# A sinkhorn attention and gated MLP kernel on one core: one q turned by a transposing transfer, a new order of all units, output products in halves

## The chip, the core and the metric

The kernel runs on one core of one Trainium2 chip. The metric is the device time of one execution in microseconds (us). A core has five engines with their own instruction streams: TensorE (PE in the profile, with its weight loads as PEld), VectorE (DVE), ScalarE (ACT), GpSimd (POOL) and SyncE (SP). SP, ACT and POOL also issue transfers, which sixteen DMA engines carry out. Each engine works through its own instructions in program order and waits at one whose inputs or buffers are not ready.

## What is computed

With B=4 batches, H=8 heads, S=768 tokens, D=64 and 8 blocks of 96 tokens:

```python
P = sort_net                                   # (B, H, 8, 8)
for _ in range(5):                             # P = softmax-like rows, then columns
    P = np.exp(P - P.max(-1, keepdims=True))
    P = P / (P.sum(-1, keepdims=True) + 1e-9)
    P = P / (P.sum(-2, keepdims=True) + 1e-9)
k_sorted = einsum('bhij,bhjcd->bhicd', P, k_blocks)      # blocks mixed by P; v the same
scores = scale * q_block @ k_sorted_block.T              # per block of 96 tokens
x = softmax(scores) @ v_sorted_block                     # (B, S, 512) over all heads
h = relu(x @ w_in)                                       # 512 -> 1024
u, v = h[..., :512], h[..., 512:]
v = (v - mean(v)) / sqrt(var(v) + 1e-6)
v = einsum('ts,bsd->btd', w_spatial, v) + b_spatial      # mixes tokens, 768 x 768
out = (u * v) @ w_out                                    # 512 -> 512
```

## The kernel before

All work is cut into small units, and the string ORDER (lines 18 to 51) lists them in the order in which they are issued. A unit is a name and its arguments, parted by colons; `run` calls the function `u_<name>` for each. The schedule is manual: the list is at once the order of the instructions on each engine. The framework adds the waits that data and buffers ask for. The batches overlap in the list: while one is in the MLP, the next is in attention.

The units of one batch b, in the order in which data flows (`ps` is the number 0 to 3 of a PSUM buffer, an engine letter A, D or P says who evicts or computes, hp is a pair of heads, ih a half of the tokens):

- `L:q:b`, `L:k:b`, `L:v:b`, and `L:wv`, `L:wu`, `L:wsa`, `L:wsb`, `L:wo` for the weights: loads from memory, issued by POOL, casting to bf16. `LH` loads half of the first q in fp32 over SP, and `QC` casts it on ACT. Loaded tiles and the output tiles share a ring of eight buffers (`ld`).
- `SK:0` to `SK:4`: the five normalisations on ACT and DVE. `PR`, `P0`, `PC`, `PD` spread P over the partitions, on PE, DVE, ACT or DVE, and POOL.
- `KT` (L383, 12 matmuls with 64-column weights): a pair of heads of k is mixed and turned. `VT` does the same for v of batch 0, and `VB` (L401) turns it back. For other batches `VM` (L410) mixes v into the tile `vm`, and `VC` (L423) copies four 16-row pieces into `vb` by SP transfers.
- `QT` and `QQ` (L314): one or two pairs of heads of q are turned by PE transposes, 12 or 24 with 64-column weights, and copied to `qT` by ACT or DVE.
- `SC` (L442): 8 score matmuls with 64-row weights, then an exponential on ACT (L447) into a ring of five tiles. `AT` (L488): 8 matmuls of the exponentials with `vb`, then reciprocal and product on DVE (L495, L496).
- `XT` (L518): x turned by PE transposes, or `XD` (L506): turned by one transposing transfer on SP (batches 2 and 3).
- `VP` (L554) and `UP` (L597): the two halves of `x @ w_in`, evicted with relu. `ST` (L571) statistics on DVE, `LN` on ACT, `LA` (L583) normalisation on DVE. `WW` (L531) turns the spatial weights once.
- `SP` (L609): 12 matmuls that mix tokens, then the sum with the bias on DVE (L615, tile `z`, three buffers). `GT` (L626): the gate product with u on DVE or POOL.
- `OP` (L635): two 128-token rows of the output product, `OE` evicts them, `OS` stores them. For the last batch `SH`, `GH`, `OH`, `OI`, `OJ` are smaller pieces of `SP`, `GT`, `OP`, `OE`, `OS`.
- `DM` (L226): six dummy matmuls at the start. `CK`, `CF`, `LF`: a check that all sums lie in a safe range, its flag, and the loading of that flag by the engines; behind `IF` the list's tail runs in the usual branch (else a general path, not taken here).

Two functions in the kernel are not in the list before. `QP` copies one pair of heads of q within SBUF so that both heads of a token group lie side by side, and `QX` turns them all at once:

```python
def u_QX(b, lo, hi):                                        # L368
    nc.sync.dma_start_transpose(
        out=q_tile(b)[:, lo * S:hi * S].rearrange("p (x c) -> p x c", c=128),
        in_=st["qp", b][:, lo:hi].rearrange("p k g h d -> p (k g h d)"))
```

`OP` has a last argument `parts`; with 2, each row's 512 columns are made as two products of 256 (L635): `for c in range(0, DM, w): for mc in range(FC): matmul(t[:, x, c:c + w], ...)`.

Of the kernel before, what the change touches and what calls it, by code (L numbers as in the profile page):

```python
# [15 lines left out]


ORDER = """
IV:0 CO S0 SK:0 SK:1 LH:S:0 L:q:0:4:8 L:k:0:0:8 L:v:0:0:8 SK:2 IV:2 ID MA L:v:1:0:8 MC QC:A:1 SK:3 L:k:1:0:8 MB QC:A:0
DM:0:6:512 L:q:1:0:8 DM:2:6:512 DM:1:6:512 QT:3:A:0:1 SK:4 QT:2:A:0:3 DM:0:6:512 DM:3:6:512 L:wv QT:1:A:0:0 QT:2:A:0:2  # L20
PR:0 P0:0:2 L:wu P0:6:8 P0:2:4 DM:3:6:512 P0:4:6 PC:D KT:1:D:0:1 PD:1:4:8 KT:3:A:0:0 L:wsb L:wsa KT:0:D:0:3 KT:2:A:0:2
IV:1 L:v:2:0:8 VT:1:A:0:0 VT:3:D:0:1 PD:1:0:4 SC:0:0:0:0 SC:2:0:0:1 VB:1:D:0:0 L:k:2:0:8 VB:3:D:0:1 SC:0:0:1:0
VT:1:A:0:2 AT:2:0:0:0 VT:3:A:0:3 PD:2:4:8 AT:0:0:1:0 L:q:2:0:8 VM:1:A:1:0 VB:2:D:0:2 SC:3:0:1:1 XT:0:D:0:0:0
AT:1:0:0:1 SC:2:0:2:0 VM:3:A:1:3 VB:0:D:0:3 PD:2:0:4 SC:1:0:2:1 AT:2:0:2:0 KT:3:D:1:1 KT:0:D:1:2 SC:1:0:3:0 VM:2:A:1:1
SC:3:0:3:1 AT:1:0:1:1 KT:2:A:1:3 KT:0:A:1:0 AT:3:0:3:0 VM:1:A:1:2 PD:3:4:8 QQ:2:D:1:0 XT:3:D:0:1:0 L:k:3:0:8
AT:0:0:3:1 XT:1:A:0:0:2 QQ:2:A:1:2 AT:3:0:2:1 VP:1:A:0:0:1 XT:0:D:0:1:2 ST:0:1 VP:2:D:0:2 ST:0:0 SC:0:1:1:1 SC:3:1:2:1
L:q:3:0:8 VC:1:4:8 VP:1:D:0:4:5 SC:2:1:3:1 ST:0:4 ST:0:5 SC:3:1:3:0 VP:0:A:0:3 SC:2:1:0:1 ST:0:2 UP:1:A:0:1:1
AT:0:1:1:1 L:v:3:0:8 SC:3:1:0:0 ST:0:3 UP:2:A:0:0:0 AT:0:1:3:1 AT:1:1:2:1 LN:0:0:6 UP:3:A:0:0:1 AT:0:1:0:1 LA:0:5
WW:2:A:0 WW:1:D:4 XT:3:A:1:1:2 UP:0:A:0:1:0 LA:0:2 VC:1:0:4 AT:2:1:0:0 VM:1:A:2:1 BI WW:3:D:2 SC:0:1:2:0 VM:2:A:2:2
XT:1:D:1:1:0 LA:0:0 BH LA:0:4 LA:0:1 LA:0:3 VM:3:A:2:0 SC:0:1:1:0 VP:1:A:1:4:5 AT:2:1:3:0 AT:0:1:1:0 ST:1:5 SP:3:0:2  # L30
AT:0:1:2:0 L:wo SP:1:0:0 VM:2:D:2:3 SP:0:0:1 VC:2:4:8 XT:3:D:1:0:2 XT:1:A:1:0:0 VC:2:0:4 QQ:2:D:2:0 KT:0:A:2:1
KT:3:D:2:0 GT:D:0:0 QQ:1:D:2:2 KT:2:A:2:2 KT:0:A:2:3 PD:3:0:4 GT:P:0:2 VP:3:A:1:0:1 SC:1:2:0:1 SC:2:2:0:0 SP:0:0:3
ST:1:4 SC:3:2:2:1 SC:1:2:1:1 ST:1:1 VP:2:A:1:2:3 KT:3:D:3:2 QQ:0:D:3:0 ST:1:2 SC:1:2:3:0 UP:2:A:1:1:0 AT:0:2:0:1
GT:P:0:3 KT:3:A:3:0 ST:1:3 QQ:1:D:3:2 SC:0:2:3:1 AT:2:2:2:1 UP:3:D:1:0:1 VM:1:A:3:3 UP:0:A:1:0:0 AT:2:2:3:1
UP:3:A:1:1:1 GT:P:0:1 ST:1:0 LN:1:0:6 AT:2:2:1:1 AT:0:2:3:0 XD:2:1 LA:1:4 OP:1:0:0:2 AT:2:2:0:0 OE:A:0:0 OP:0:0:2:2
SC:2:2:2:0 LA:1:2 LA:1:5 OE:D:0:2 SC:1:2:1:0 LA:1:1 LA:1:0 LA:1:3 OP:3:0:4:2 AT:1:2:1:0 AT:0:2:2:0 SP:2:1:2 VM:0:D:3:1
VM:1:D:3:0 OE:A:0:4 VP:3:D:2:4:5 KT:0:A:3:1 KT:2:D:3:3 SP:1:1:3 VM:0:A:3:2 GT:D:1:3 OS:0:0 ST:2:4 SP:3:1:1 SC:2:3:3:1
SC:1:3:1:1 XD:2:0 OS:0:2 GT:D:1:2 ST:2:5 SP:0:1:0 VC:3:4:8 SC:3:3:2:1 SC:2:3:0:1 UP:1:D:2:1:0 GT:D:1:1 VC:3:0:4
VP:3:A:2:2:3 AT:1:3:3:1 GT:P:1:0 VP:2:A:2:0:1 ST:2:3 AT:1:3:2:1 AT:3:3:1:1 UP:0:A:2:1:1 OP:1:1:0 ST:2:0 ST:2:1 ST:2:2
OE:A:1:0 AT:2:3:0:1 LN:2:0:6 LA:2:1 UP:0:D:2:0:0 SC:1:3:0:0 LA:2:3 SC:3:3:1:0 LA:2:2 LA:2:5 LA:2:0 OP:2:1:4 AT:1:3:0:0  # L40
AT:3:3:1:0 XD:3:1 OE:A:1:4 OP:0:1:2 LA:2:4 SC:1:3:3:0 OE:D:1:2 SC:3:3:2:0 SP:2:2:2 AT:1:3:2:0 UP:0:A:2:0:1 AT:3:3:3:0
CK VP:2:A:3:4:5 GT:D:2:2 OS:1:2 SP:1:2:1 ST:3:5 OS:1:4 XD:3:0 SP:3:2:3 SP:2:2:0 ST:3:4 CF:3 GT:D:2:1 GT:P:2:3
UP:0:A:3:1:0 VP:2:D:3:2:3 VP:3:A:3:0:1 ST:3:0 ST:3:1 ST:3:2 UP:2:A:3:0:1 GT:P:2:0 LF OP:1:2:2 ST:3:3 OE:A:2:2 LN:3:0:6
OP:0:2:0 LA:3:4 LA:3:5 OS:2:2 OE:A:2:0 UP:3:D:3:1:1 LA:3:2 LA:3:0 OP:2:2:4 LA:3:3 OE:A:2:4 LA:3:1 OS:2:4 UP:0:A:3:0:0
SH:1:3:3:0 GH:P:3:3:0 SH:2:3:0:0 GH:D:3:0:0 SH:0:3:1:0 SH:2:3:2:0 SH:3:3:1:1 GH:P:3:1:0 SH:1:3:0:1 GH:P:3:2:0 OS:1:0
GH:P:3:1:1 SH:2:3:3:1 SH:3:3:2:1 OS:2:0 GH:P:3:0:1 GH:D:3:2:1 GH:D:3:3:1 OS:0:4 IF OH:1:3:2:0:512:0:4
OH:2:3:3:0:512:0:4 OH:0:3:4:0:256:0:4 OI:A:3:2:0:512 OI:A:3:3:0:512 OH:3:3:5:0:256:0:4 OI:D:3:4:0:256 OI:D:3:5:0:256
OJ:3:2:0:512:S OJ:3:3:0:512:S OJ:3:4:0:256:S OJ:3:5:0:256:A OH:2:3:5:256:512:0:4 OH:1:3:1:0:512:0:4
OH:3:3:4:256:512:0:4 OI:D:3:5:256:512 OI:A:3:1:0:512 OJ:3:5:256:512:S OI:A:3:4:256:512 OJ:3:4:256:512:S OJ:3:1:0:512:A
OH:2:3:0:0:512:0:4 OI:A:3:0:0:512 OJ:3:0:0:512:S  # L50
"""


# [773 lines left out]
```

## Time and profile before

| | |
|---|---|
| time, median of 3 runs | 156.74 us (156.48 to 156.78) |
| profiled execution, its own time | 156.77 us |
| span of that execution | 155.0 us |
| PE busy | 148.5 us (96%) |
| DVE busy | 120.3 us (78%) |
| ACT busy | 81.6 us (53%) |
| POOL busy | 36.8 us (24%) |
| granted TensorE clock | 1.0 |

The span runs from the first to the last instruction of the core; the execution's time has 1.77 us around it. The profile is read through a page (busy time of each engine, the span in 40 slices, the chain of work that ended last, the costliest groups of instructions) and through views of the same trace: the chain in order of time, instructions in order of time, groups by shape, transfers with their time from issue to landing. In the group rows stand the line, engine and operation, the tiles out<-in, the count, the busy time in all, the mean of one in ns, and the engine's idle time ahead of them. PE times in the instruction rows overlap, because matmuls are pipelined; the chain's pieces do not.

### The profile page before, as it was taken

What the parts mean: (1) busy time and instruction counts of PE and PEld (TensorE: products, weight loads), DVE (VectorE), ACT (ScalarE), POOL (GpSimd) and SP (SyncE); (2) the same over time, 40 slices, a digit from 0 to 9 for tenths busy, and PEclk for the clock granted to TensorE, in tenths of its full rate; (3) what the DMA queues carried; (4) which work ended last, traced back from release to release, by engine and by line L of the source; (5) the groups of instructions that cost most, each with busy time, mean ns of one, the idle gap of its engine ahead of it and who ended that gap; (6) DMA issues with size and microseconds to landing.
All of it is one profiled execution on the core that took longest, in us unless ns stands there. A gap on an engine that the chain in (4) does not pass through costs nothing.

```text
span 155.0 us, 4028 instructions
## 1 busy us (share of the span) xinstructions
PE 148.5 (96%) x1689; PEld 92.1 (59%) x1689; DVE 120.3 (78%) x261; ACT 81.6 (53%) x112; POOL 36.8 (24%) x43
## 2 busy tenths in 40 slices
PE   6999898999999999999999999999999999999990
...
GB/s 72 267 203 204 205 204 205 208 217 238 271 217 203 203 204 204 242 226 16 0 17 224 43 198 64 147 1 4 102 148 185 44 0 0 131 49 371 141 226 183
DMA packets 27653, 23.57 MB, mean 152 GB/s; under 512 B 7280, under 2 KB 24688, under 8 KB 27632
## 3 DMA queue, kind: packets, MB, share of 16 engines
...
q10 hardware_dynamic: 288, 0.39, 0.7%
q8 instruction: 14, 0.23, 0.6%
...
## 4 chain that ended last, share of the span: by engine, by line
PE 93%; ACT 3%; DVE 1%; issue 1%; DVEq 0%; ACTq 0%
PE ps L609 15%; PE ps L554 14%; PE ps L597 14%; PE ps L635 10%; PE ps L226 7%; PE ps L488 5%; PE ps L665 5%; PE ps L442 4%; PE ps L383 4%; PE ps L314 4%; PE ps L685 3%; PE ps L410 2%; PE ps L518 2%; PE ps L531 1%; PE ps L401 1%; ACT kt_all L115 1%
## 5 line engine op out<-in xcount | busy, mean ns | idle before, releaser
L447 ACT ACTIVATE ex_all<-ps 96x768 bf16<-96x768 f32 x32 | 24.8, 805 | 8.7 <-PE ps L442 8.6
L626 POOL TENSOR_TENSOR gt<-z,u_sb 128x768 bf16<-128x768 f32 x6 | 9.8, 1642 | 78.6 <-DVE z L615 61.3
L609 PE MATMUL ps<-wspT,v_sb 128*128 128x384 bf16 x144 | 25.1, 326 | 0.0
L597 PE MATMUL ps<-xT,w_in_sb 128*128 128x384 bf16 x128 | 23.5, 326 | 0.0
L554 PE MATMUL ps<-w_in_sb,xT 128*128 128x512 bf16 x96 | 22.9, 380 | 0.2 <-issue 0.2
L496 DVE TENSOR_TENSOR x_sb<-ps,rec_all 96x512 bf16<-96x512 f32 x32 | 22.0, 687 | 1.1
L609 PEld LDWEIGHTS <-v_sb 128*128 128x128 bf16 x144 | 13.5, 98 | 8.9
L571 DVE BATCH_NORM_STATS2 stats<-v_sb 128x6 f32<-128x512 bf16 x24 | 16.3, 678 | 2.0 <-ACT v_sb L121 1.5
L115 ACT COPY o_sb<-ps 128x1024 f32<-128x1024 f32 (+2 forms) x12 | 9.7, 816 | 15.2 <-PE ps L685 10.2
L635 PE MATMUL ps<-w_out_sb,gt 128*128 128x256 bf16 (+1 forms) x96 | 16.9, 326 | 0.0
L615 DVE TENSOR_TENSOR z<-ps,b_bc 128x768 f32<-128x768 f32 x12 | 11.4, 952 | 7.0 <-PE ps L609 6.8
L121 ACT ACTIVATE u_sb<-ps 128x768 bf16<-128x768 f32 x12 | 9.7, 810 | 13.1 <-PE ps L597 13.0
L597 PEld LDWEIGHTS <-w_in_sb 128*128 128x128 bf16 x128 | 11.6, 98 | 7.4
L554 PEld LDWEIGHTS <-xT 128*128 128x128 bf16 x96 | 8.6, 98 | 9.7 <-issue 0.7
L121 ACT ACTIVATE v_sb<-ps 128x1024 bf16<-128x1024 f32 (+1 forms) x9 | 8.8, 976 | 9.1 <-PE ps L554 9.1
L488 PEld LDWEIGHTS <-ex_all 96*128 96x128 bf16 x256 | 10.6, 97 | 3.7 <-issue 0.6
L488 PE MATMUL ps<-vb,ex_all 96*128 96x65 bf16 x256 | 12.2, 193 | 0.5 <-issue 0.5
L635 PEld LDWEIGHTS <-gt 128*128 128x128 bf16 x96 | 9.0, 98 | 5.5
L226 PE MATMUL ps<-warm 128*128 128x512 bf16 x36 | 10.7, 461 | 1.3 <-DVE warm L201 1.3
L115 ACT CAST kt_all<-ps 128x768 bf16<-128x768 f32 x9 | 6.9, 800 | 6.5 <-PE ps L383 6.5
L442 PE MATMUL ps<-qT,kt_all 64*128 64x96 bf16 x256 | 9.3, 204 | 0.4 <-DVE kt_all L117 0.4
L495 DVE RECIPROCAL rec_all<-ps 96x8 f32<-96x8 f32 x32 | 6.3, 196 | 4.3 <-PE ps L488 4.0
...
## 6 DMA issues: line engine op xcount, KB each, us to landing
...
k_in<-in_k_dram POOLq DMA_DIRECT2D x4, 768.0 KB, 23.2
v_in<-in_v_dram POOLq DMA_DIRECT2D x4, 768.0 KB, 22.3
vb<-vm SPq DMA_DIRECT2D x24, 99.0 KB, 5.8
q_in<-in_q_dram POOLq DMA_DIRECT2D x3, 768.0 KB, 29.8
...
q<-in_q_dram SPq DMA_DIRECT2D x1, 768.0 KB, 4.6
```

What stands on the lines that cost most here:

```text
L115: nc.scalar.copy(out=out, in_=in_)
L121: nc.scalar.activation(out=out, in_=in_, func=AF.Relu)
L226: nc.tensor.matmul(t[:, 0, 0:int(w)], lhsT=warm[:, 0:128], rhs=warm[:, 0:int(w)], start=True, stop=True)
L442: nc.tensor.matmul(t[:, hh, 0:HW].rearrange("p (g x) -> p g x", g=G)[:, :, ii * TB:(ii + 1) * TB], lhsT=kT[rows, i * BLK:i * BLK + 128], r ...
L447: nc.scalar.activation(out=e_tile(b, hp, ih).rearrange("p h (x g) -> p h x g", g=G), in_=t[0:BLK, :, 0:HW].rearrange("p h (g x) -> p h x g ...
L488: nc.tensor.matmul(t[:, hh, ii * VW:ii * VW + D + 1], lhsT=e[:, c:c + 128], rhs=vb[b % 2][:, ih * NI + ii, 2 * hp + hh, 0:D + 1], start=Tr ...
L496: nc.vector.tensor_mul(out=x_sb[:, hp].rearrange("p i (h d) -> p h i d", h=2), in0=tv[:, :, :, 0:D], in1=_raw_ap(rec, 0, [rec.ap[0], [NI, ...
L554: nc.tensor.matmul(t[:, x, :], lhsT=st["xT", b][:, n // 3, kc, (n % 3) * 128:(n % 3 + 1) * 128], rhs=w_in_sb[:, kc, DH:DFF], start=(kc == ...
L571: nc.vector.bn_stats(out=stats, in_=st["v_sb", b, n])
L597: nc.tensor.matmul(t[:, x, 0:HW], lhsT=w_in_sb[:, kc, mc * 128:(mc + 1) * 128], rhs=st["xT", b][:, ih, kc, :], start=(kc == 0), stop=(kc = ...
L609: nc.tensor.matmul(t[:, x, 0:HW], lhsT=st["v_sb", b, n][:, mc * 128:(mc + 1) * 128], rhs=wspT[:, 3 * x:3 * x + 3, n, :], start=(n == 0), s ...
L635: nc.tensor.matmul(t[:, x, c:c + w], lhsT=st["gt", b, mc][:, (n0 + x) * 128:(n0 + x + 1) * 128], rhs=w_out_sb[:, mc, c:c + w], start=(mc = ...
```

## The change

Only the list changes. Batch 3's q is no longer turned by `QQ:0:D:3:0` and `QQ:1:D:3:2`; four `QP:A:3:*` on ACT and one `QX:3:0:4` on SP take their place. All nine `OP` units have parts=2 (before, the three of batch 0). All other units remain, in a new order, many with another PSUM buffer or engine: of the gate products `GT`, ten are on POOL and two on DVE (before six and six), of the `GH` seven and one (before five and three), of the `KT` evictions twelve on ACT and four on DVE (before nine and seven). The q, k, v loads come in another order as well.

```diff
-IV:0 CO S0 SK:0 SK:1 LH:S:0 L:q:0:4:8 L:k:0:0:8 L:v:0:0:8 SK:2 IV:2 ID MA L:v:1:0:8 MC QC:A:1 SK:3 L:k:1:0:8 MB QC:A:0
-DM:0:6:512 L:q:1:0:8 DM:2:6:512 DM:1:6:512 QT:3:A:0:1 SK:4 QT:2:A:0:3 DM:0:6:512 DM:3:6:512 L:wv QT:1:A:0:0 QT:2:A:0:2
-PR:0 P0:0:2 L:wu P0:6:8 P0:2:4 DM:3:6:512 P0:4:6 PC:D KT:1:D:0:1 PD:1:4:8 KT:3:A:0:0 L:wsb L:wsa KT:0:D:0:3 KT:2:A:0:2
...
+S0 CO LH:S:0 SK:0 L:q:0:4:8 SK:1 IV:0 SK:2 L:v:0:0:8 QC:A:0 SK:3 DM:0:6:512 DM:1:6:512 L:k:0:0:8 ID L:k:1:0:8 MC
+L:v:1:0:8 SK:4 DM:3:6:512 DM:0:6:512 L:q:1:0:8 MA L:wv QT:3:A:0:0 QC:A:1 BH QT:0:A:0:3 IV:2 DM:1:6:512 L:wu QT:2:A:0:2
+L:wsb MB IV:1 PR:1 P0:6:8 DM:3:6:512 P0:0:2 P0:2:4 P0:4:6 L:wsa PC:A PD:1:4:8 PD:1:0:4 VT:0:A:0:0 QT:3:D:0:1 L:k:2:0:8
+VT:1:A:0:1 VB:0:D:0:0 VT:2:A:0:2 KT:3:A:0:2 VB:1:D:0:1 KT:2:D:0:3 VT:0:A:0:3 SC:3:0:2:0 L:v:2:0:8 VB:1:D:0:2
+SC:2:0:3:0 VB:0:D:0:3 KT:3:A:0:1 SC:1:0:2:1 KT:2:D:1:3 KT:3:A:0:0 L:q:2:0:8 KT:0:D:1:2 KT:1:A:1:1 AT:2:0:2:0
+SC:3:0:0:1 PD:2:4:8 AT:0:0:3:0 SC:1:0:3:1 SC:2:0:1:1 AT:3:0:0:1 SC:1:0:1:0 AT:0:0:3:1 PD:2:0:4 AT:2:0:2:1 VM:3:A:1:0
+VM:1:A:1:1 VM:0:D:1:3 KT:2:A:1:0 AT:3:0:1:1 L:q:3:0:8 VM:1:A:1:2 L:k:3:0:8 XT:0:A:0:1:2 QQ:2:D:1:2 SC:1:0:0:0
+QQ:3:D:1:0 XT:0:A:0:1:0 PD:3:4:8 AT:1:0:0:0 L:v:3:0:8 SC:2:1:2:0 SC:3:1:0:1 VP:0:A:0:3 AT:1:0:1:0 SC:2:1:3:0
+VP:3:D:0:4:5 XT:2:D:0:0:2 VC:1:0:4 XT:0:A:0:0:0 UP:1:A:0:0:1 ST:0:5 VC:1:4:8 ST:0:4 SC:3:1:1:0 VP:2:A:0:0:1 ST:0:3
+AT:0:1:3:0 AT:1:1:1:0 VP:3:A:0:2 ST:0:0 UP:2:A:0:0:0 ST:0:2 SC:0:1:0:0 AT:3:1:2:0 UP:1:A:0:1:1 ST:0:1 LN:0:0:6
+WW:2:D:2 SC:3:1:3:1 AT:0:1:0:1 LA:0:2 LA:0:4 LA:0:0 LA:0:1 WW:1:A:4 UP:2:A:0:1:0 AT:3:1:0:0 KT:0:A:2:3 WW:1:D:0
+KT:2:A:2:2 KT:0:D:2:1 SC:3:1:2:1 XT:1:D:1:0:2 KT:2:A:2:0 XT:0:D:1:0:0 VM:3:D:2:0 VM:1:A:2:2 LA:0:3 LA:0:5 BI
+VM:2:A:2:1 VP:0:A:1:0:1 AT:3:1:2:1 AT:2:1:3:1 SP:1:0:1 VM:2:A:2:3 QQ:0:D:2:0 L:wo XT:3:D:1:1:2 SC:1:1:1:1 QQ:2:A:2:2
+SC:0:2:1:1 QP:A:3:2 QP:A:3:0 AT:3:1:1:1 SP:1:0:3 XT:3:A:1:1:0 GT:P:0:1 SP:0:0:0 VC:2:4:8 SC:3:2:2:0 SC:2:2:3:1
+VP:1:D:1:4:5 SC:2:2:1:0 ST:1:4 SC:0:2:0:1 ST:1:5 ST:1:1 VC:2:0:4 PD:3:0:4 UP:3:A:1:0:1 GT:D:0:0 SP:1:0:2 KT:2:A:3:2
+GT:P:0:2 KT:3:A:3:3 UP:0:D:1:1:0 QP:A:3:1 VM:2:A:3:0 VM:1:A:3:2 ST:1:0 VP:3:A:1:2:3 GT:P:0:3 QP:A:3:3 QX:3:0:4
+AT:1:2:1:0 AT:0:2:3:1 UP:2:A:1:1:1 AT:1:2:2:0 VM:3:A:3:3 ST:1:3 OP:0:0:0:2 ST:1:2 AT:1:2:1:1 OE:A:0:0 LN:1:0:6
+UP:2:A:1:0:0 AT:0:2:0:1 VM:3:A:3:1 OP:1:0:2:2 SC:2:2:2:1 LA:1:4 VC:3:4:8 LA:1:3 SC:3:2:3:0 LA:1:1 LA:1:0 LA:1:5
+OP:0:0:4:2 OE:D:0:2 OE:A:0:4 LA:1:2 AT:2:2:2:1 SC:1:2:0:0 XD:2:1 SP:3:1:0 KT:1:A:3:0 KT:0:A:3:1 SP:2:1:2 AT:1:2:3:0
+AT:3:2:0:0 SP:0:1:1 SC:1:3:0:1 SC:2:3:1:1 VP:3:D:2:4:5 GT:P:1:0 ST:2:4 SC:0:3:2:1 SC:2:3:1:0 VC:3:0:4 XD:2:0 SP:1:1:3
...
+XD:3:1 OP:1:1:4:2 LA:2:1 OE:D:1:2 AT:2:3:0:0 AT:3:3:2:0 OE:A:1:4 SP:0:2:0 GT:P:2:0 AT:3:3:3:0 SP:1:2:3 VP:2:A:3:4:5
+SP:0:2:2 XD:3:0 UP:3:D:3:0:1 ST:3:5 CK VP:1:A:3:0:1 SP:2:2:1 VP:3:A:3:2:3 ST:3:4 CF:2 ST:3:3 GT:P:2:3 ST:3:0 GT:P:2:2
+ST:3:2 ST:3:1 OS:1:2 UP:0:A:3:1:1 GT:P:2:1 LF OP:3:2:4:2 LN:3:0:6 LA:3:2 OP:0:2:0:2 UP:1:A:3:1:0 OP:2:2:2:2 OE:D:2:4
...
+SH:3:3:3:1 SH:1:3:1:1 GH:P:3:1:1 GH:P:3:3:1 OS:2:0 IF OH:0:3:2:0:512:0:4 OH:3:3:3:0:512:0:4 OI:A:3:2:0:512
...
+OJ:3:1:0:512:S OJ:3:5:256:512:A OI:D:3:4:256:512 OH:2:3:4:0:256:0:4 OI:D:3:4:0:256 OJ:3:5:0:256:S OJ:3:4:256:512:A
+OJ:3:4:0:256:A
```

More of the change, by code (lines that the diff above doesn't have):

```diff
@@ L24 @@
[L24 to L48, printed above, removed]
```

11 lines of the change are left out of this document (7 added, 4 removed).

## The prediction

> **What bounds the kernel now.** I read the page first (busy shares, then the 40 slices), then the chain of waits in order of time, then the instructions of the stretches where that chain leaves TensorE (PE).
>
> ```profile
> span 155.0 us, 4028 instructions
> ...
> PE 148.5 (96%) x1689; PEld 92.1 (59%) x1689; DVE 120.3 (78%) x261; ACT 81.6 (53%) x112; POOL 36.8 (24%) x43
> ...
> PE   6999898999999999999999999999999999999990
> ...
> PE 93%; ACT 3%; DVE 1%; issue 1%; DVEq 0%; ACTq 0%
> ```
>
> The first row is the span, the next the busy times; in the slices PE has a hole only at both ends and around the fourth and sixth slice; the last row gives it 93% of the chain. So a unit's time on PE counts in full, and other engines count only where PE waits for them. The chain shows the places:
>
> ```profile
> 12.33 1.40 PE ps L226 x6
> ...
> 14.57 1.50 ACT kt_all L115 x2
> ...
> 25.49 0.81 ACT ex_all L447
> ...
> 33.71 0.34 PE ps L518 x8
> ...
> 40.30 0.24 PE ps L488 x8
> ...
> 61.16 0.67 PE ps L314 x24
> ...
> 71.93 0.24 PE ps L488 x8
> ...
> 73.29 0.28 PE ps L442 x8
> 73.57 0.35 PE ps L488 x8
> 73.92 1.30 PE ps L597 x8
> ...
> 78.88 1.75 PE ps L635 x16
> ...
> 104.69 1.73 PE ps L635 x8
> ...
> 130.57 3.45 PE ps L635 x16
> ...
> 146.15 5.21 PE ps L685 x32
> 151.37 0.02 issue
> 151.39 0.58 ACT o_sb L115
> ```
>
> Columns are start, length, engine and line. Until 27 us evictions on ACT and DVE alternate with PE; from there to 151.37 every piece is PE. Two things are read off for the sum. A unit has a fixed price (eight L488 matmuls 0.24, a 24-matmul q turn 0.67, eight L597 1.30). And a change between the units with 64-row or 64-column weights (L383 and L314, or L442) and the rest costs 0.11 more: L488 takes 0.24 at 71.93, but 0.35 at 73.57, straight behind L442. The Trainium skill, "TensorEngine Tiling (Array Packing)", Key Properties, says that changing the tiling mode drains the TensorE; the two L488 rows agree, and no figure is taken from the page.
>
> I add these prices in the order of the list and call the sum ahead of a unit its position. For the list before, XT:0:D:0:1:2 has position 27.47 and starts at 33.71 (offset 6.24); the first OH has 139.68 and starts at 146.15 (6.47). Over 112 us the addition and the trace differ by 0.23, so the same addition for the new list is worth having.
>
> **The change, part by part.**
>
> *Two double q turns leave PE.* QQ:0:D:3:0 and QQ:1:D:3:2 are 24 transposes each: 2 x 0.67 = -1.34.
>
> *Output products in halves.* Three of nine are in halves already: 1.75 for 16 matmuls (78.88) against 1.73 for 8 (104.69). Six more: 6 x 0.02 = +0.12. Nothing else hangs on a half, since the four products of each half read the same tiles in the same order.
>
> *New order.* Counting the changes of weight shape along both lists gives 65 before and 72 after: 7 x 0.11 = +0.77. All other PE units are the same in kind and number, the 36 dummy matmuls included. So the positions end at 144.86 before and 144.41 after: **-0.45**, a third of what the removed turns seemed to give.
>
> *What the turn needs instead.* Four QP copies on ACT, one transposing transfer on SP, one more tile of the eight-deep load ring.
>
> ```profile
> L117 DVE COPY qT<-ps 128x1536 bf16<-128x1536 bf16 x5 | 4.7, 948 | 0.3 <-PE ps L314 0.2
> ...
> L115 ACT COPY qT<-ps 128x768 bf16<-128x768 bf16 x4 | 3.1, 789 | 1.4 <-PE ps L314 1.4
> ```
> ```profile
> xT<-x_sb SPq DMA_TRANSPOSE x4, 3.8
> ```
> ```profile
> 117.73 1.65 SPq L506 DMA_TRANSPOSE xT<-x_sb  x1
> ```
>
> A QP copies 128x768 bf16 within SBUF, which no row shows; the nearest is 789 ns from PSUM, so 4 x 0.79 = 3.2 us of ACT, while DVE loses two evictions of 948 ns. Neither is on the path: ACT is busy 53% of the span. QX moves 128x3072 elements where an XD moves 96x2048, twice as many: between 3.8 us and 2 x 3.8 = 7.6, of which up to 2 x 1.65 = 3.3 block SP; I take 7.6. By positions, QP:A:3:3 can start at 69 and the first score of batch 3, SC:1:3:0:1, is at 86.16: 17 us of PE work cover it. What stands behind QX on SP (VC:3:4:8) waits for VM:3:A:3:1 at position 73.9 anyway. If that cover were gone, the whole 7.6 would show. Cost 0. The Trainium skill, "VectorE: DVE Perf Modes", The three transpose paths, speaks against the transfer: 390 ns for a 128x128 block on TensorE, 1309 ns through the DMA, and the advice to use TensorE where PSUM will do. At 24 blocks in a row it would make 31 us, an estimate from that page, and PE would wait 31 - 17 = 14.
>
> The ring tile takes the slot of the spatial weights, whose last transposition (WW:1:A:4, position 38.9) lies 14 us ahead of the first QP: 0.
>
> *The q load must be there when ACT comes to QP.* ACT would stand still otherwise, and every eviction behind it.
>
> ```profile
> 29.76 0.94 POOL L171 DMA_DIRECT2D k_in<-in_k_dram  x1
> ```
> ```profile
> k_in<-in_k_dram POOLq DMA_DIRECT2D x1, 768.0 KB, 28.0
> ```
>
> The fourteenth load of the queue landed at 29.76 + 28.0 = 57.8 (the rate is that of the queue, so the place in the order decides). In the new list q of batch 3 is the fourteenth. QP:A:3:2 comes on ACT behind the eviction of QQ:2:A:2:2 (PE done at position 52.5) and an exponential, at 54.7, near 61: 3 us to spare, cost 0.
>
> *Head (to 34 us).* The value turns come first, and 24 evictions stand on ACT from VT:0:A:0:0 to the score SC:3:1:0:1.
>
> ```profile
> 20.26 0.80 ACT L115 CAST vT<-ps 128x768 bf16<-128x768 f32 x1 [0.47 <-PE ps L383]
> 20.95 0.81 ACT L115 CAST vm<-ps 128x768 bf16<-128x768 f32 x1
> ```
> ```profile
> 13.40:33.00 19.60, 18.00 (x392) 13.83 (x391) 16.55 (x31) 16.15 (x21) 11.71 (x13) 1.00 1.29 206
> ```
>
> Each lasts 0.80, but the next begins 0.69 later when it is ready, so 24 take between 24 x 0.70 = 16.8 and 24 x 0.80 = 19.2; before, this stretch held 21 on ACT (busy 16.15 us) and 31 instructions on DVE. One q turn fewer stands ahead of PR, so the first VT starts at 12.33 + 1.40 - 0.34 = 13.4, its eviction at 13.9. Following PE, ACT and DVE unit by unit with these steps, and the PSUM buffers, ACT is the last in nearly every wait and itself waits 2.3 to 2.6 us for PE: VP:3:D:0:4:5 (position 27.11) starts at 13.9 + 16.8 + 2.3 = 33.0, up to 33.3, an offset of 5.9 to 6.2 against 6.24. Ends: without any of those waits 30.7 (3.6), at 0.80 an eviction with half of them 34.2 (7.1). I take 6.0, from the 0.69 row: **-0.24**.
>
> *Three places where the new list is tight.* (a) The value copies of batch 1:
>
> ```profile
> 29.90 0.72 SPq L423 DMA_DIRECT2D vb<-vm  x1
> ```
> ```profile
> 31.95 1.24 SPq L423 DMA_DIRECT2D vb<-vm  x2
> ```
> ```profile
> vb<-vm SPq DMA_DIRECT2D x2, 99.0 KB, 8.0
> ```
>
> The fourth transfer, issued at 31.95, lands 8.0 later, at 39.95, and the first reader ran at 40.30 (chain). Now VM:1:A:1:2 is evicted near 28.9, the fourth lands near 39.0, and AT:0:1:3:0 (position 33.04) comes at 39.0: 0 to 0.4, I take 0.1. (b) Positions 41 to 46: KT and WW of different shapes follow each other on the same PSUM buffers, with only 0.10 to 0.54 between the end of an eviction and the next writer; the tightest before were 0.05 and 0.10. 0 to 0.5, I take 0.2. (c) The end of batch 2:
>
> ```profile
> 122.40 0.96 DVE L615 TENSOR_TENSOR z<-ps,b_bc 128x768 f32<-128x768 f32 x1
> 123.53 1.64 POOL L626 TENSOR_TENSOR gt<-z,u_sb 128x768 bf16<-128x768 f32 x1 [22.88 <-DVE z L615]
> ```
> ```profile
> 126.20 0.14 DVE L727 CAST flag<-ends 1x1 int32<-1x1 f32 x1
> ...
> 133.33 0.69 DVE L571 BATCH_NORM_STATS2 stats<-v_sb 128x6 f32<-128x512 bf16 x1 [0.46 <-issue]
> ```
>
> All four gates are now on POOL. SP:2:2:1 ends at position 120.45; 0.96 and 1.64 and two hand-overs of 0.1 later, at 123.3, the last gate is there, and OP:3:2:4:2 wants it at 123.58. The flag, 4.2 us ahead of its reader before (126.34 to 130.57), is written near 122.8, and reading it (0.46 on DVE) ends near 123.3 too. 0 to 0.7, I take 0.1. Together **+0.40**.
>
> *Tail.*
>
> ```profile
> 152.00 0.33 SPq L697 DMA_DIRECT2D out_dram<-o_sb  x1
> ```
> ```profile
> L115 ACT COPY o_sb<-ps 128x512 f32<-128x512 f32 x4 | 2.3, 585 | 10.2 <-PE ps L685 10.2
> ...
> L117 DVE COPY o_sb<-ps 128x256 f32<-128x256 f32 x3 | 1.2, 425 | 0.9 <-PE ps L685 0.9
> ```
>
> The last eviction is a half row on DVE, 425 ns for 585, its store behind two others on ACT's queue: between -0.16 and +0.2, I take **-0.10**.
>
> The other moved steps (loads on POOL's queue, gates, statistics) I cost at nothing: PE is continuous there before, 50 units of the old list are marked for DVE and 36 of the new, and the least distance from an eviction to the next writer of its buffer after position 60 is 0.38 in the new list (at the OP of (c)) and 0.21 in the old.
>
> **Sum**: -0.45 - 0.24 + 0.40 - 0.10 = -0.39, against the profiled execution's 156.77 (span 155.0 and 1.77 around it): 156.38. That execution is 0.03 above the median of 156.74, so **156.4**.
>
> **The rivals.** *No new waits.* Without the 0.40 and with an offset of 5.9, 155.9. For it: DVE, the busier helper, is relieved. Against: each of the three places needs everything punctual.
> *The edges eat the saving.* Each costs double what I took: 156.8. This is no measurable change; from no change this kernel's runs (156.48 to 156.78) can tell about 0.2%, 0.31 us.
> *Slower: ACT paces the head.* Place: 14 to 33 us. If an eviction steps at 0.76 to 0.80, as when each waits for its matmul, the offset becomes 6.7 to 7.1: +0.9 in the middle, 157.3. It decides from a step of 0.76 on. For it: 21 evictions kept ACT 16.15 of 19.60 us. Against: the step of 0.69.
> *Slower: the end of batch 2.* PE waits 0.9 instead of 0.1 for gate or flag, because DVE reaches the last z late: 157.2; it decides from 0.8. For it: 0.28 us of margin where there were 4. Against: before, reading the flag left no gap on PE at 130.57.
> *The transfer is late.* It decides where its landing takes over 17 us, more than four times an XD. Against: an XD of 16 blocks of 96x128 lands in 3.8 us. By the 1309 ns a block of the Trainium skill, "VectorE: DVE Perf Modes", The three transpose paths, the time would be 156.4 + 14 = 170; 16 blocks would take 21 us there, and the measured 3.8 speaks against it.
>
> **How the numbers follow.** Forecast 0.32; no new waits 0.11; edges 0.22; ACT-paced head 0.20; end of batch 2 0.11; transfer or q late, or a wait I have not seen, 0.04. Faster 0.32 + 0.11 = 0.43, same 0.22, slower 0.20 + 0.11 + 0.04 = 0.35. The range reaches from the no-waits case with a head 0.4 faster (ACT waiting less) to both slower cases partly together: 155.5 to 157.9.
>
> **What would show it.** L314 with 48 matmuls fewer; L635 96 more of 256 columns, 48 fewer of 512; no PE wait at the first score of batch 3 and a landing of the new transfer under 8 us; VP of tiles 4 and 5 at 33.0 (34 or later means the ACT-paced head); PE waits at 39, 47 to 52 and 130 of 0.1 to 0.2. Wrong it would be by any PE gap over 0.5 us after 34, above all at OP of batch 2, or by ACT standing at the first QP.

## The result

The changed kernel takes 157.18 us (median of 20 runs, 156.69 to 158.28), the kernel before 156.52 (20 runs, 156.44 to 156.96): a ratio of 1.0045, 95% interval 1.0027 to 1.0063. It is 0.45% slower, 0.66 us; the forecast was 156.4, faster. The time lies inside the range.

The profiled execution of after took 157.20 us, that of before 156.77. From the page of after (busy times, the slices, the shares of the chain):

```profile
span 155.4 us, 4042 instructions
...
PE 147.0 (95%) x1679; PEld 96.0 (62%) x1689; DVE 110.3 (71%) x247; ACT 87.8 (56%) x122; POOL 45.9 (30%) x49
...
PE   6979988999999999999999999999999999999990
...
PE 78%; DVE 10%; ACT 6%; issue 2%; DMA 1%; DVEq 0%; ACTq 0%
```

PE is busy 1.5 us less than before, and yet the span grew by 0.4. The 1.5 us do not measure the work that went: 1.2 of them lie with the dummy matmuls at the start (10.7 us busy in before, 9.5 in after), and ten of after's matmul records are missing (1679 beside 1689 weight loads). By the positions the work fell by 0.45. The chain of waits of after, in order of time, shows where it leaves PE:

```profile
11.10 0.23 DVE p_t L252
...
25.14 0.57 issue
...
33.65 1.83 PE ps L555 x8
...
95.53 2.07 PE ps L610 x12
97.70 0.96 DVE z L616
98.66 0.12 DVE rec_all L496
98.80 0.69 DVE x_sb L497
99.49 1.70 DVE gt L627
...
102.13 0.70 DVE x_sb L497
102.87 0.35 PE ps L443 x8
...
146.33 5.21 PE ps L686 x32
151.62 0.42 DVE o_sb L118
```

Three places are to be seen: a row "issue" of 0.57 in the head, a stretch of DVE between 97.70 and 102.87 in the middle of PE's row, and the end. Laid against the positions of the prediction (VP of tiles 4 and 5 at 27.11, the SP that starts at 95.53 at 88.9, the first OH at 139.23), the offset is 33.65 - 27.11 = 6.54, then 6.63, then 7.10. So most of the 0.5 us of the body is lost between 95.5 and 103 us; on both sides of that stretch the sum of unit prices and of 0.11 us a switch holds to 0.1 us.

The account of the two profiled executions, before to after:

| part | us |
|---|---|
| PR starts sooner (11.97, then 11.47, where it waits for p_t) | -0.50 |
| PE work from PR on, by positions | -0.12 |
| stands from PR to VP of tiles 4 and 5 (before: to XT), 2.44, then 2.91 | +0.47 |
| stands from there to the first OH, 0.23, then 0.56 | +0.33 |
| from the first OH to the end of the span, 8.85, then 9.07 | +0.22 |
| sum | +0.40 |

The pieces of the chain start up to 0.16 us later than the same instructions in their own rows (146.33 and 146.17); below, where a start stands against another, both are from the same view. In the nine profiled executions of kernels with after's head PR starts between 11.47 and 11.82, so an account of two single executions is good to some tenths of a us.

### The profile page after: what moved, and what is told of

It is laid out like the page before. It is cut to its first block, busy times and chain, and to the rows that moved or that the text cites. A ratio compares the mean times of both kernels' runs of the same rounds, so it can differ in the third digit from the quotient of the medians.

```text
span 155.4 us, 4042 instructions
## 1 busy us (share of the span) xinstructions
PE 147.0 (95%) x1679; PEld 96.0 (62%) x1689; DVE 110.3 (71%) x247; ACT 87.8 (56%) x122; POOL 45.9 (30%) x49
## 4 chain that ended last, share of the span: by engine, by line
PE 78%; DVE 10%; ACT 6%; issue 2%; DMA 1%; DVEq 0%; ACTq 0%
PE ps L610 15%; PE ps L555 12%; PE ps L598 12%; PE ps L636 10%; PE ps L666 5%; PE ps L489 4%; PE ps L443 4%; PE ps L686 3%; PE ps L384 3%; ACT ex_all L448 2%; PE ps L411 2%; PE ps L315 2%; PE ps L519 2%; ACT kt_all L116 1%; PE ps L532 1%
## 5 line engine op out<-in xcount | busy, mean ns | idle before, releaser
L627 POOL TENSOR_TENSOR gt<-z,u_sb 128x768 bf16<-128x768 f32 x10 | 17.1, 1714 | 74.6 <-DVE z L616 59.4
L555 PE MATMUL ps<-w_in_sb,xT 128*128 128x512 bf16 x87 | 22.3, 380 | 0.6
L122 ACT ACTIVATE v_sb<-ps 128x1024 bf16<-128x1024 f32 (+1 forms) x10 | 9.4, 939 | 15.1 <-PE ps L555 15.1
L636 PE MATMUL ps<-w_out_sb,gt 128*128 128x256 bf16 x144 | 16.9, 273 | 0.0
L636 PEld LDWEIGHTS <-gt 128*128 128x128 bf16 x144 | 13.8, 98 | 2.2
L116 ACT COPY o_sb<-ps 128x1024 f32<-128x1024 f32 (+2 forms) x10 | 8.1, 820 | 12.5 <-issue 8.1
L122 ACT ACTIVATE u_sb<-ps 128x768 bf16<-128x768 f32 x13 | 10.6, 812 | 7.9 <-PE ps L598 7.7
L489 PEld LDWEIGHTS <-ex_all 96*128 96x128 bf16 x256 | 10.7, 97 | 4.0 <-issue 0.7
L116 ACT CAST kt_all<-ps 128x768 bf16<-128x768 f32 x12 | 9.4, 803 | 3.4 <-PE ps L384 3.3
L227 PE MATMUL ps<-warm 128*128 128x512 bf16 x35 | 9.5, 425 | 1.3 <-DVE warm L202 1.3
L443 PE MATMUL ps<-qT,kt_all 64*128 64x96 bf16 x256 | 10.0, 205 | 0.5 <-DVE x_sb L497 0.4
```

The costliest lines, as they stand in the source:

```text
L116: nc.scalar.copy(out=out, in_=in_)
L122: nc.scalar.activation(out=out, in_=in_, func=AF.Relu)
L443: nc.tensor.matmul(t[:, hh, 0:HW].rearrange("p (g x) -> p g x", g=G)[:, :, ii * TB:(ii + 1) * TB], lhsT=kT[rows, i * BLK:i * BLK + 128], r ...
L489: nc.tensor.matmul(t[:, hh, ii * VW:ii * VW + D + 1], lhsT=e[:, c:c + 128], rhs=vb[b % 2][:, ih * NI + ii, 2 * hp + hh, 0:D + 1], start=Tr ...
L555: nc.tensor.matmul(t[:, x, :], lhsT=st["xT", b][:, n // 3, kc, (n % 3) * 128:(n % 3 + 1) * 128], rhs=w_in_sb[:, kc, DH:DFF], start=(kc == ...
L627: eng.tensor_mul(out=gt, in0=st["z", b, mc], in1=u)
```

## The experiments

Ratios and medians stand against runs of the kernel before on the same chip (156.55 to 156.72 us).

**The gate product.** In after, DVE's gate of column 2 of batch 2 runs beside two gates of POOL. Instructions of after in order of time, first DVE, then POOL:

```profile
99.41 1.78 DVE L627 TENSOR_TENSOR gt<-z,u_sb 128x768 bf16<-128x768 f32 x1
```
```profile
98.73 3.95 POOL L627 TENSOR_TENSOR gt<-z,u_sb 128x768 bf16<-128x768 f32 x2 [8.47 <-DVE z L616]
```

```diff
-AT:3:3:1:1 UP:0:A:2:0:0 GT:D:1:2 GT:P:1:3
+AT:3:3:1:1 UP:0:A:2:0:0 GT:P:1:2 GT:P:1:3
```

> The kernel after with the one gate product of batch 2 that VectorE computes, column 2, given to GpSimd (its z is there from 91.4 us, so GpSimd can compute it there, alone, before the gates at 98.7 us). Theory of the gates: after's stall around 103 us comes from VectorE's gate, 1.78 us at 99.41 beside two gates of GpSimd (3.95 us at 98.73) where GpSimd's gate at 88.62 took 1.65 alone; without it GpSimd's two gates at 98.7 take 3.3 us in place of 3.95, the reciprocal now at 101.93 starts near 100.2, the scores now at 102.87 start at 102.3 to 102.5, all later positions come 0.4 to 0.5 us earlier, the time is 156.7 to 156.8. Rival, the loss between 95 and 103 us is no wait for VectorE at all: the scores stay at 102.8 to 102.9 and the time at 157.2.

Measured: 157.03 us (ratio 1.0033, 1.0014 to 1.0053). POOL computes the moved gate at 91.67, and its pair is back at its price:

```profile
98.94 3.24 POOL L627 TENSOR_TENSOR gt<-z,u_sb 128x768 bf16<-128x768 f32 x2 [5.63 <-DVE z L616]
```

The scores start at 102.60 in an execution whose head was 0.20 later; from VP of tiles 4 and 5 to the first OH it is 112.27 us in place of 112.58. So the stretch was the gates', and it is worth 0.31 us in the trace. Two kernels below that differ by this gate alone (the bias in eight transfers, without and with it) show the same, 112.58 and 112.26. Of the 0.4 to 0.5 that I expected in the time the medians show 0.15, within what they can tell. Two gates side by side cost both engines: 0.95 became 1.78 on DVE, 3.24 became 3.95 on POOL. The Trainium skill, "SBUF — State Buffer", "Who interferes with whom", says that a DVE instruction with two SBUF inputs and a GpSimd instruction that reads SBUF take turns at one shared port; these rows agree.

**The branch hint.** `BH` had moved from the middle of the list to its head, which the prediction passed over.

```diff
-QT:3:A:0:0 QC:A:1 BH QT:0:A:0:3
+QT:3:A:0:0 QC:A:1 QT:0:A:0:3
...
-VM:1:A:2:2 LA:0:3
+VM:1:A:2:2 BH LA:0:3
```

> The kernel after with the branch hint (a PE, VectorE and ScalarE instruction, at the head of the order in after) put back among the transposes of the spatial weights, where before has it. Theory of the hint: the early hint makes the 0.57 us in which PE stood at 25.14 with nothing in the profile that released it, and the spread of after's times up to 158.28; without it no such stand of over 0.3 us before 45 us, the time 156.6 to 156.8, no run over 157.5. Rival, the hint does nothing: a stand of 0.4 to 0.6 us stays in the head, the time is 157.0 to 157.3, and runs of about 158.2 still come up.

Measured: 157.26 us (ratio 1.0054, 1.0030 to 1.0078), a stand of 0.57 us at the same unit, and three of eight runs at 158.3. The hint does nothing; that theory fell. The execution profiled here was one of those of 158.3, and is used below.

**Is the head paced by evictions?** Twice: evictions moved to DVE, then taken from ACT and given to nobody.

```diff
-VT:2:A:0:2  KT:3:A:0:1  VM:1:A:1:1
+VT:2:D:0:2  KT:3:D:0:1  VM:1:D:1:1
```

> The kernel after with three evictions of the head given from ScalarE to VectorE (the mixed values of heads 4 and 5, the mixed keys of heads 2 and 3 of batch 0, the values of heads 2 and 3 of batch 1). Theory that ScalarE paces the head (it was busy 4.00 of 4.00 us in 20 to 24): ScalarE has 2.4 us less to do, the value products of token tiles 4 and 5 of batch 0, now at 33.66, start at 33.1 to 33.4, and the time is 156.7 to 156.9. Rival, the head's loss lies in PE's own stands that nothing released (0.57 us at 25.14): the value products stay within 0.15 us of 33.66 and the time within 0.2 of 157.2; with VectorE's 0.95 us for an eviction in place of 0.80 it may even be 0.2 later.

Measured: 158.24 us (ratio 1.0107, 1.0088 to 1.0127), VP of tiles 4 and 5 at 34.27. Neither theory's numbers came true: DVE is no freer there than ACT, and PE now waits for its evictions of kt_all (0.4), vm (0.4) and vT (0.3).

The second kernel copies, for KT of batch 0 and VM of batch 1 (pairs 0 and 1 of each), only a few columns; POOL sets the rest to 0 or 1 beforehand:

```diff
-copy(e, to[:, x], of[:, x])
+copy(e, to[:, 0:8], of[:, 0:8])
...
-copy(eng, vm[:, :, 2 * hp:2 * hp + 2, 0:D].rearrange(...), t[:, :, 0:G * D].rearrange(...))
+copy(eng, vm[:, 0:1, 2 * hp:2 * hp + 2, 0:D].rearrange(...), t[:, :, 0:D].rearrange(...))
```

> The kernel after, with four of ScalarE's evictions of the head (the mixed keys of heads 0 to 3 of batch 0, the values of heads 0 to 3 of batch 1) cut to a few columns: the rest of these tiles is not copied and holds constants set by GpSimd, so the outputs are not the reference's. That takes some 2 us off ScalarE between 18 and 29 us and gives them to nobody. Theory that evictions pace the head: the value products of token tiles 4 and 5 of batch 0, at 33.66 in after, start at 32.9 to 33.3, the time falls by 0.3 to 0.7. Rival, the head is paced by the arrival of loads and PE's fetching of code: 33.5 to 33.8, and the time within 0.2 us of after's 157.2.

Measured: 157.37 us (ratio 1.0061, 1.0039 to 1.0083). Busy times in 20 to 24 us (columns: stretch, length, PE, PEld, DVE, ACT, POOL, clock), after and then the lightened head, and PE's stop in each:

```profile
20.00:24.00 4.00, 3.57 (x96) 3.04 (x96) 3.25 (x6) 4.00 (x7) 0.88 (x1) 1.00 1.32 206
```
```profile
20.00:24.00 4.00, 3.46 (x96) 3.00 (x96) 3.22 (x6) 3.18 (x5) 0.88 (x1) 1.00 1.32 206
```
```profile
25.71 0.27 PE L489 MATMUL ps<-vb,ex_all 96*128 96x65 bf16 x3 [0.57 <-issue]
```
```profile
25.71 0.27 PE L494 MATMUL ps<-vb,ex_all 96*128 96x65 bf16 x3 [0.54 <-issue]
```

ACT, busy 4.00 of 4.00 before, has 0.8 us of slack now, and PE's rows agree within 0.04 us up to the stop at 25.71. Only behind it come 0.27 us (VP of tiles 4 and 5 at 33.32 against 33.59). So these four evictions pace 0.27 us of the head, all of it behind the stop, and the medians show no gain from that.

**The two parts of the change alone, in the order of before.** First the turn: four copies and one transfer in the place of the two double transposes.

```diff
-KT:3:D:3:2 QQ:0:D:3:0 ST:1:2 SC:1:2:3:0 UP:2:A:1:1:0 AT:0:2:0:1
+KT:3:D:3:2 QP:A:3:0 ST:1:2 SC:1:2:3:0 UP:2:A:1:1:0 QP:A:3:2 AT:0:2:0:1
...
-ST:1:3 QQ:1:D:3:2 SC:0:2:3:1
+ST:1:3 QP:A:3:1 SC:0:2:3:1
...
-VM:1:A:3:3 UP:0:A:1:0:0
+VM:1:A:3:3 QP:A:3:3 QX:3:0:4 UP:0:A:1:0:0
```

> The kernel before in its own order, whose two double transposes of batch 3's q (the ones evicted by VectorE between the scores of batch 2) are replaced by four copies on ScalarE and one transposing transfer at PE position 68. Theory of the sum: PE loses 1.34 us of work and nothing waits, as the copies (0.79 us each) and the transfer (5.6 us in after) end 17 us or more before the first scores of batch 3: 155.1 to 155.4. Rival, ScalarE's 3.2 us more of copies come among the exponentials of batch 2 and delay their scores: 155.7 to 156.2. Rival on the other side, the transposes were done in time in which PE waited anyway: 156.4 to 156.7.

Measured: 157.28 us (ratio 1.0041, 1.0028 to 1.0053): slower than before by 0.7, outside every expectation. PE's instructions in order of time:

```profile
70.24 1.46 PE L597 MATMUL ps<-xT,w_in_sb 128*128 128x384 bf16 x8 [0.38 <-ACT v_sb L121]
...
72.96 0.34 PE L442 MATMUL ps<-qT,kt_all 64*128 64x96 bf16 x8 [0.56 <-DVE x_sb L496]
...
74.02 1.46 PE L597 MATMUL ps<-xT,w_in_sb 128*128 128x384 bf16 x8 [0.36 <-ACT kt_all L115]
```

The 1.34 us of transposes are gone, and 1.30 us of stands have come at the same place: the transposes were the work between an eviction and the next use of its PSUM tile. (The 0.7 us of the profiled execution: PR starts 0.33 later in it, and 0.43 lie behind PE's last product, see the end of the program.) Then the same with the copies at 79 to 84 us, out of the way:

```diff
-OP:1:0:0:2 AT:2:2:0:0 OE:A:0:0 OP:0:0:2:2
+OP:1:0:0:2 QP:A:3:0 QP:A:3:1 AT:2:2:0:0 OE:A:0:0 OP:0:0:2:2 QP:A:3:2
...
-OE:D:0:2 SC:1:2:1:0
+OE:D:0:2 QP:A:3:3 QX:3:0:4 SC:1:2:1:0
```

> As the run with the turn alone (157.28 us), but the four copies on ScalarE moved from 68 to 75 us to the output products of batch 0 at 79 to 84 us, and the transfer behind them; PE's order is the same. Theory of the spacing: the three stands of PE at 70.24, 72.96 and 74.02 in that run (0.38, 0.56 and 0.36 us) come from PSUM tiles that are written again too soon once the double transposes between them are gone; they stay, within 0.15 us each, and the time is 157.1 to 157.4. Rival, ScalarE's copies delay the evictions: the stands behind ScalarE (0.38 and 0.36) go and the time is 156.4 to 156.7.

Measured: 157.28 us (ratio 1.0039, 1.0026 to 1.0053). The stands of 0.38 and 0.56 stay to the hundredth. The third goes, so that one was the copies', and another of 0.31 comes at 84.82, behind an exponential that now waits for a copy. Then the units of 69 to 76 us in an order that keeps the distances:

```diff
-SC:1:2:3:0 UP:2:A:1:1:0 AT:0:2:0:1 GT:P:0:3 KT:3:A:3:0 ST:1:3 SC:0:2:3:1 AT:2:2:2:1 UP:3:D:1:0:1 VM:1:A:3:3 UP:0:A:1:0:0
+SC:1:2:3:0 UP:0:A:1:1:0 AT:2:2:0:1 GT:P:0:3 KT:3:A:3:0 ST:1:3 UP:1:D:1:0:1 SC:0:2:3:1 AT:2:2:2:1 VM:3:A:3:3 UP:1:A:1:0:0
```

> As the run before it (turn alone, copies late), with the units of 69 to 76 us of the kernel before put in another order and on other PSUM tiles, so that on PE at least 0.3 us lie between an eviction's end and the tile's next use, but for one place with none. Theory of the spacing: the stands fall from 1.30 us in all to 0.3 or less, the work saved arrives, and the time is 155.4 to 155.9, under both kernels. Rival, the units between are paced by VectorE or ScalarE as a whole, whatever the order: stands of 0.8 us or more stay and the time is 156.4 to 157.3.

Measured: 156.67 us (ratio 1.0000, 0.9990 to 1.0009): the three stands are gone, the one of 0.31 (at 84.23) is left, the first OH starts at 145.48, 0.51 earlier than before (0.26 of it because PR starts earlier in this execution), and the span is only 0.1 shorter. From the KT at 69.05 to the two AT at 78.23 of before PE takes 8.20 us in place of 9.18: of the 1.34 us, 0.98 arrive there, and 0.31 go again at 84.23. The mechanism was right, the time was missed by 0.8, of which 0.4 lies behind PE's last product.

The halves alone:

```diff
-OP:1:1:0   OP:2:1:4   OP:0:1:2   OP:1:2:2   OP:0:2:0   OP:2:2:4
+OP:1:1:0:2 OP:2:1:4:2 OP:0:1:2:2 OP:1:2:2:2 OP:0:2:0:2 OP:2:2:4:2
```

> The kernel before in its own order, with the six output products of batches 1 and 2 that run over all 512 columns split in halves of 256 like those of batch 0. Theory of the sum: 0.02 us each (1.75 for 1.73), 0.12 us in all on PE and nothing else: 156.6 to 156.8. Rival, the halves cost more because each half loads its weights again and PE is stopped more often to fetch its code (192 instructions more): 157.0 or more. Rival, an output product gives way to something: 156.4 or less.

Measured: 156.69 us against 156.72 (ratio 1.0002, 0.9993 to 1.0011). The halves cost nothing that can be told from 0.12. (There are 96 instructions more, 48 products and 48 weight loads, not 192.)

**The end of the program.** What SyncE waited for at the end (us in total, times, longest), in before, in after and in the kernel with the turn alone:

```profile
SPq L822 <- DMA out_dram<-o_sb: 1.0, 2, 0.8
```
```profile
SPq L823 <- DMA out_dram<-o_sb: 2.5, 1, 2.5
```
```profile
SPq L822 <- DMA out_dram<-o_sb: 1.4, 1, 1.4
```

(In after the last three stores go out from ACT, and SyncE has issued its own by 151.27, so it stands longer.) In the re-spaced kernel, too, it is one stand of 1.4, though its PE, evictions and stores follow each other just as in before. One transfer more is common to all that have it. So one transfer was added to before, and nothing else:

```diff
-nc.sync.dma_start(out=b_bc, in_=_raw_ap(moe_b_spatial, 0, [[0, 128], [1, S]]))
+for p in range(0, 128, 64):
+    nc.sync.dma_start(out=b_bc[p:p + 64], in_=_raw_ap(moe_b_spatial, 0, [[0, 64], [1, S]]))
```

> The kernel before, with the bias loaded by two transfers of 64 partitions in place of one of 128: one transfer more in SyncE's list and nothing else. The transfers of the hardware queues take eight completion counters in turn, and the program ends with SyncE waiting for them one after the other; in before the last store has the eighth counter, in after and in the runs with the turn alone (which have one transfer more) the first. Theory of the ring: with the last store on the first counter the waits for the others come behind it; the stand of SyncE at the end is one of 1.4 us as in those runs, in place of 0.8 and a short one, the span grows by 0.3 to 0.45 us with PE's end where it was, the time is 156.9 to 157.1. Rival, the longer end comes from the transposing transfer or the stores themselves: the time stays at 156.5 to 156.75.

Measured: 156.98 us against 156.56 (ratio 1.0029, 1.0017 to 1.0041), with the row as expected:

```profile
SPq L823 <- DMA out_dram<-o_sb: 1.4, 1, 1.4
```

Its first OH even starts 0.28 earlier than before's; the 0.4 lie wholly behind PE. The trace also records each wait. The transfers that SyncE and ACT issue raise eight counters in turn, and SyncE waits for them one after the other, about 0.06 us apart. In before there are 48 such transfers: the last store, landed at 154.00, raises the counter that is waited for last, and SyncE's closing drain starts at 154.08. Here there are 49: the last store lands at 153.73 on the counter waited for first, seven waits follow, and the drain starts at 154.23. From that landing to the end of the span it is 0.97 us in before and 1.39 here.

And after with seven transfers more (the same lines with pieces of 16 partitions):

> The kernel after, with the bias loaded by eight transfers of 16 partitions in place of one: seven transfers more, so that the last store has the eighth counter again, as in before. Theory of the ring: the end of the program is 0.3 to 0.45 us shorter, the time 156.7 to 156.9 (after: 157.18). Rival, the end is long because three stores of after end behind each other on ScalarE's queue: the time stays at 157.1 to 157.3.

```profile
SPq L824 <- DMA out_dram<-o_sb: 2.1, 4, 0.8
```

Measured: 156.93 us (ratio 1.0038, 1.0017 to 1.0059). The profiled execution is 155.13 - 146.34 = 8.79 from the first OH to the end, 0.42 less than after's 155.38 - 146.17 = 9.21. The time fell by 0.25, a little less than expected, and its interval alone would not tell it from after's. With the gate on POOL as well:

> The kernel after with both: the bias in eight transfers and the gate product of column 2 of batch 2 on GpSimd (the run with the gate alone gave 157.03, its profiled body 0.31 us less). If the two are independent: 157.18 less 0.3 to 0.45 less 0.15 to 0.31, so 156.4 to 156.7, level with before. If the ring does nothing: 157.0.

Measured: 156.40 us (ratio 1.0003, 0.9977 to 1.0029), level with before, as expected if both count. It is 0.78 under after, while the two alone gave 0.25 and 0.15; what makes the rest isn't shown.

**Both together on the re-spaced kernel**, with two copies moved forward:

```diff
-KT:3:A:3:0 UP:1:D:1:0:1
+KT:3:A:3:0 QP:A:3:2 UP:1:D:1:0:1
...
-VM:3:A:3:3 UP:1:A:1:0:0
+VM:3:A:3:3 QP:A:3:3 UP:1:A:1:0:0
...
-OP:1:0:0:2 QP:A:3:0 QP:A:3:1 AT:2:2:0:0
+OP:1:0:0:2 QP:A:3:0 QP:A:3:1 QX:3:0:4 AT:2:2:0:0
...
-OP:0:0:2:2 QP:A:3:2
+OP:0:0:2:2
...
-OE:D:0:2 QP:A:3:3 QX:3:0:4 SC:1:2:1:0
+OE:D:0:2 SC:1:2:1:0
...
-nc.sync.dma_start(out=b_bc, in_=_raw_ap(moe_b_spatial, 0, [[0, 128], [1, S]]))
+for p in range(0, 128, 16):
+    nc.sync.dma_start(out=b_bc[p:p + 16], in_=_raw_ap(moe_b_spatial, 0, [[0, 16], [1, S]]))
```

> The re-spaced kernel with the turn by one transfer (156.67), with two of its four copies moved forward into stands of ScalarE at 72.8 and 75.2 us and the transfer behind the other two, so that no exponential of 82 to 84 us comes behind a copy (the stand of 0.31 us at 84.23 goes), and the bias in eight transfers, so that the last store has the eighth counter. By the spacing and the ring: 156.67 less 0.3 less 0.3 to 0.45, so 155.9 to 156.1, under before by 0.5 or more. If the ring does nothing: 156.3 to 156.5. If the places of the copies do not matter either: 156.6 to 156.8.

Measured: 155.81 us against 156.56 (ratio 0.9952, 0.9939 to 0.9965). It is faster than both kernels. The first OH starts at 144.97, 1.02 earlier than in before (PR 0.17 earlier), and the last row is before's again:

```profile
SPq L823 <- DMA out_dram<-o_sb: 1.0, 2, 0.9
```

So the turn by one transfer is worth 0.75 us of its 1.34 us of PE work, once the work around it keeps its distances and the end its order.

**The upper part of the spread.** Of the 72 runs of kernels with after's head 17 lie some 1.1 us higher, with a granted clock of 0.986 to 0.989; of 117 with before's head none has a clock under 0.99. (Two of the 72 are as high at a clock of 1.0, 158.02 in after and 157.94 with the gate on POOL; they stay unexplained.) The hint run profiled such an execution. Busy time of PE and its clock in two stretches of 3.4 us there (columns: stretch, length, PE, clock, transfers):

```profile
22.30:25.70 3.40, 2.53 (x61) 1.00 1.32 205
25.70:29.10 3.40, 3.33 (x28) 0.50 1.26 205
```

From 25.7 to 29.1 us the clock is half. The first stretch in after's profiled execution and in before's:

```profile
22.30:25.70 3.40, 2.47 (x59) 1.00 1.31 204
```
```profile
22.30:25.70 3.40, 3.31 (x72) 1.00 1.32 205
```

PE works there 73% of the time in after and 97% in before. Two kernels fill the stretch with multiplications of zeros:

```diff
-SC:3:0:0:1
+DM:3:1:512 SC:3:0:0:1
...
-SC:1:0:3:1
+DM:1:1:512 SC:1:0:3:1
...
-AT:3:0:0:1
+DM:3:1:512 AT:3:0:0:1
```

The second has `DM:3:2:512`, `DM:1:2:512` and `DM:3:2:512` there.

> The kernel with the ring and the gate product mended (156.40 us; 3 of its 12 runs at 157.6 to 157.9 with a granted clock of 0.987 to 0.989), with three multiplications of zeros of 128x512 (0.22 us each) put into PE's list of the head, ahead of units at 22.4, 23.2 and 23.9 us, where PE stands 0.16 us at a time. Theory of the gate: the clock is halved for 3.4 us where PE was busy too little of the 3.4 us before (2.47 of 3.40 in 22.3 to 25.7 in after, 3.31 in before); with 0.65 us more of work in that stretch few or none of the runs have a clock under 0.99, at a price of 0 to 0.3 us in the others: median 156.3 to 156.6, highest under 157.2. Rival, the halved clock does not hang on PE's work in the head: about a quarter of the runs still lie 1.1 us higher with a clock of 0.986 to 0.989.

> The same with six such multiplications, two at each of the three places, 1.3 us of work. Theory of the gate: no run with a clock under 0.99, at a price of 0.4 to 0.9 us: median 156.8 to 157.2, the highest within 0.6 of the lowest. Rival: a quarter of the runs still 1.1 us higher with a clock of 0.986 to 0.989.

Measured: 156.92 us (ratio 1.0029, 1.0018 to 1.0041; 156.59 to 157.29) and 157.16 (1.0049, 1.0031 to 1.0067; 157.05 to 157.94). PE's busy time in the stretch rose to 3.05 and 3.23:

```profile
22.30:25.70 3.40, 3.05 (x61) 1.00 1.31 204
```
```profile
22.30:25.70 3.40, 3.23 (x59) 1.00 1.32 204
```

None of the twelve runs has a clock under 0.998. At 17 in 72, twelve runs without one would come up by chance 4 times in 100; so the theory of the gate is favoured, not proved. Against 156.40 the price was larger than expected for the first, 0.5 us, and as expected for the second, 0.8; the second's highest run, 157.94 with a clock of 1.0, stays unexplained too, and lies outside the spread that was expected.

## Why the prediction was wrong

The forecast was -0.39 against before's profiled execution, and after's lies at +0.43. Of these 0.82 us the head makes 0.54, the tail 0.32 and the body -0.07; the rest is rounding.

**PE work, -0.45: right.** The positions of the new list hold within 0.1 us from 33.65 to 95.53.

**Head, offset 6.0 taken, 6.54 measured: this step failed.** Not by the evictions that it followed: the term lacks PE's stop of 0.57 at 25.14, which no eviction releases and the lightened head left where it was. In the profiled execution of the kernel with ring and gate mended it hardly shows. PE's weight loads at that place, in after and in that kernel:

```profile
25.70 0.15 PEld L489 LDWEIGHTS <-ex_all 96*128 96x128 bf16 x3 [0.69 <-issue]
```
```profile
25.57 0.14 PEld L490 LDWEIGHTS <-ex_all 96*128 96x128 bf16 x3 [0.20 <-issue]
```

There PR to VP took 21.64 us (11.82 to 33.46) in place of 22.12, so the evictions' share was about as reckoned. Before had stops of its own (0.47 and 0.18), which its offset of 6.24 contained and my walk of the new list did not carry over. The prediction doesn't mention them; one of them is the size of the whole forecast gain. The rival of the ACT-paced head gave 157.3, the nearest of all; but its mechanism isn't what happened: with four of ACT's evictions lightened PE's rows up to the stop stayed where they were. Nor does its lower bound follow from its own working: with a step of 0.76 and half of ACT's waits it is 13.9 + 18.2 + 1.15 = 33.3, an offset of 6.2 and not 6.7.

**Places (a), (b), (c), +0.40: nothing was lost there.** AT:0:1:3:0 has offset 6.54, VP:0:A:1:0:1 behind the cluster 6.59, OP:3:2:4:2 at the end of batch 2 7.11, each the offset that PE had before it.

**"The other moved steps I cost at nothing": this step failed too.** 0.47 us were lost behind 95.5, most of them up to 103 around a gate product, one of the moved steps: 0.31 by the run with that gate on POOL. The rows of before showed the danger (shortest, median and longest of the DVE gates in ns):

```profile
L626 DVE TENSOR_TENSOR gt<-z,u_sb x6: 936/954/1643, 62.3 to 126.3; 128x768 bf16<-128x768 f32 x6
```

The longest ran beside a gate of POOL; PE did not wait for it there. What makes the other 0.16 stays open; it is less than the 0.23 by which the addition itself missed in before. That the two errors in the body nearly cancel (0.40 expected, 0.47 lost elsewhere) is luck.

**Tail, -0.10: wrong, +0.22.** I looked at the length of the last eviction and at the queue of its store, not at what the added transfer does to the last waits: +0.4 in the run with one transfer more alone. Without it the end is 0.19 shorter than before's (8.79 in after with eight transfers, 154.97 - 145.99 = 8.98 in before), so the sign of the term was right.

**The turn and the halves: right.** The copies took 0.82 to 0.85 each, the transfer landed in 5.6 us, no PE wait stands at the first score of batch 3, ACT didn't stand at the first copy. SP was blocked 3.71, over the bound of 3.3. The halves cost nothing that shows. The rows of after, the copies (shortest, median and longest in ns), the transfer's blocking and its landing:

```profile
L116 ACT COPY qp<-q_in x4: 823/831/845, 61.2 to 75.6; 128x768 bf16<-128x768 bf16 x4
```
```profile
76.45 3.71 SPq L371 DMA_TRANSPOSE qT<-qp  x1
```
```profile
qT<-qp SPq DMA_TRANSPOSE x1, 5.6
```

The estimate of 31 us from the Trainium skill, "VectorE: DVE Perf Modes", The three transpose paths, is refuted for this transfer by the 5.6.

Of the 0.66 us between the medians the profiled executions show 0.43; the rest is that before's profiled execution lay 0.25 above its median of 20 runs.
